# A decode block that reads 256 MB: a new load order, a re-fitted planner, and the q projection in row form

## The chip, the cores and the metric

One core of one Trainium2 chip. The metric is the device time of one execution in microseconds (us), the median of several; the profile is one execution with the hardware profiler. Several chips were used in turn, so every comparison is with the kernel before run in the same rounds on the same chip.

In the profile's lines PE is the tensor engine, PEld its weight loads, DVE VectorE, ACT ScalarE, and SPq the queue that issues the loads. `<-` names what ended a wait; "issue" is idle time for which the profile shows no such end. P.V is the product of the softmax's weights with V.

## The reference, cut to what matters

```python
def _A_ref(x, k_cache, v_cache, wq, wo):          # B=4, Sq=1, Hq=32, Hkv=8, Sk=8192, Dh=128
    q = (x @ wq).reshape(B, Sq, Hq, Dh).transpose(0, 2, 1, 3)
    scores = einsum("bhqd,bhkd->bhqk", q, repeat(k_cache, 4)) * Dh ** -0.5
    o = einsum("bhqk,bhkd->bhqd", softmax(scores), repeat(v_cache, 4))
    return o.transpose(0, 2, 1, 3).reshape(B, Sq, Hq * Dh) @ wo
def _B_ref(x, w_gate, w_up, w_down):
    return (silu(x @ w_gate) * (x @ w_up)) @ w_down

x = A_x
x = x + _A_ref(layernorm(x), K, V, wq, wo);  x = x + _B_ref(layernorm(x), ...)
x = x + _A_ref(layernorm(x), K, V, wq, wo);  x = x + _B_ref(layernorm(x), ...)   # the same K, V and weights
```

Both layers read the same caches. K and V are 134 MB in bf16, far more than the 15 slots of 1 MiB that the kernel has for them, so most of it is read twice.

## The kernel before

A cache unit is 1 MiB (half of one head's K or V). The pool has 11 slots of one unit; four more slots come from wq once the last q projection is done. The kernel lays itself out with a planner: steps (a matmul group, a transpose, an eviction) with estimated durations, dependencies, PSUM banks and slots; it simulates the engines and the load queue and emits the program in the order that comes out. The load order is a string. `K` and `P` are the next one or two K units, `a110` or `A11` a V unit or pair of layer 0, `b`/`B` of layer 1, and `c110` says that layer 1 uses the unit that layer 0 left in its slot (kept, not loaded again). `KM` K units of a batch are kept over to layer 1 as well.

```python
class Plan:
    HOP = 0.06
    PAGE = 5.0          # us from one block of 256 instructions to the next
    PAGE_N = 256
    LOAD_LEAD = 2.1
    LOAD_TAIL = 2.1
    ...
                s.start = t
                dma_at = max(dma_at, t + self.LOAD_LEAD) + s.us
                s.end = dma_at + self.LOAD_TAIL
ORDER = ("c100 c101 P c260 x P c300 c301 c261 wq P wg1 c120 P c340 P K K c341 P P wo1 A06 P wo0 P a010 K c240 "
         ... )
NSLOT = 11
KM = (4, 0, 0, 0)
```

The crossing of a batch (layer 0 to layer 1: output projection, layer norm, FFN, layer norm, q) has 128 matmuls for q in two halves of 16 heads. The weights are stationary (128x128), x moves with 4 columns:

```python
for h in heads:
    for kt in range(KT):
        matmul(ps[:, bk * BW + h * B:bk * BW + (h + 1) * B],
               lhsT=wq_sb[:, kt, h * Dh:(h + 1) * Dh], rhs=xnT[:, kt * B:(kt + 1) * B],
               start=(kt == 0), stop=(kt == KT - 1))
```

Scores are line 622 of the kernel before (648 after), the K transposes 606 (632), P.V in row form 763 (789) and by columns 748 (774), the FFN 809 and 873 (835 and 899), the q projection 472 (496).

Of the kernel before, what the change touches and what calls it, by code (L numbers as in the profile page):

```python
# [115 lines left out]
class Plan:  # L116

    HOP = 0.06
    PAGE = 5.0
    PAGE_N = 256  # L120
    LOAD_LEAD = 2.1
    LOAD_TAIL = 2.1

    def __init__(self, nslots, banks):
# [11 lines left out]
    def load(self, us, fn, slots, pair=None):  # L136
        s = Step("sp", us, fn, [], [0])
        s.slot_of, s.pair = slots, pair
        self.loads.append(s)
        return s  # L140

    def run(self):
        engines = ("pe", "dve", "act")
        free_at = {e: 0.0 for e in engines}
        todo = {e: [] for e in engines}
        waits = {}
        users = {}
        for s in self.steps:
            waits[s] = len(s.deps)
            for d in s.deps:  # L150
                users.setdefault(d, []).append(s)
            if not s.deps:
                todo[s.eng].append((0.0, s))
        bank_free = {b: 0.0 for b in self.banks}
        held = {}
        slots = [(0.0, i) for i in range(self.nslots)]
        li = 0
        sp_at = 1.0
        dma_at = 0.0
        done = []  # L160

        def finish(s):
            done.append(s)
            for u in users.get(s, ()):
                waits[u] -= 1
                if waits[u] == 0:
                    t = max(d.end + (self.HOP if d.eng != u.eng else 0.0) for d in u.deps)
                    todo[u.eng].append((t, u))

        def room(s):  # L170
            if s.slot_of is None:
                return 0.0, []
            if s.pair is None:
                return min(((f, [i]) for f, i in slots), default=None)
            at = {i: f for f, i in slots}
            return min(((max(f, at[i + 1]), [i, i + 1]) for i, f in at.items()
                        if i + 1 in at and i + 1 != self.nslots), default=None)

        def pump(now):
            nonlocal li, sp_at, dma_at, slots  # L180
            while li < len(self.loads):
                s = self.loads[li]
                t = sp_at
                got = room(s)
                if got is None:
                    return
                t = max(t, got[0])
                if s.slot_of is not None:
                    if t > now:
                        return  # L190
                    slots = [x for x in slots if x[1] not in got[1]]
                    for u, i in zip((s.slot_of, s.pair), got[1]):
                        self.slot[u] = i
                s.start = t
                sp_at = t + 0.35
                dma_at = max(dma_at, t + self.LOAD_LEAD) + s.us
                s.end = dma_at + self.LOAD_TAIL
                li += 1
                finish(s)

        pe_n = 0
        page_at = 0.0

        def fetched(at, s):
            nonlocal pe_n, page_at
            if s.eng != "pe" or s.n == 0:
                return at + s.us
            first, pe_n = pe_n, pe_n + s.n
            for k in range(first // self.PAGE_N + 1, pe_n // self.PAGE_N + 1):
                there = at + s.us * (k * self.PAGE_N - first) / s.n  # L210
                at += max(0.0, page_at + self.PAGE - there)
                page_at = max(there, page_at + self.PAGE)
            return at + s.us

        self.slot = {}
        left = len(self.steps)
        pump(0.0)
        while left:
            best = None
            for e in engines:  # L220
                cand = None
                for t, s in todo[e]:
                    if s.take is not None:
                        b = min(bank_free.values()) if bank_free else None
                        if b is None:
                            continue
                        t = max(t, b)
                    at = max(t, free_at[e])
                    k = (at > free_at[e] + 1e-9, at if at > free_at[e] + 1e-9 else 0.0, s.prio[0])
                    if cand is None or k < cand[0]:  # L230
                        cand = (k, at, s)
                if cand is not None and (best is None or cand[1] < best[0]):
                    best = (cand[1], cand[2])
            nxt = None
            got = room(self.loads[li]) if li < len(self.loads) else None
            if got is not None:
                nxt = max(sp_at, got[0])
            if best is None and nxt is None:
                raise RuntimeError("the plan is stuck")
            if best is None or (nxt is not None and nxt <= best[0]):  # L240
                pump(nxt)
                continue
            at, s = best
            s.start, s.end = at, fetched(at, s)
            free_at[s.eng] = s.end
            for i, (_, x) in enumerate(todo[s.eng]):
                if x is s:
                    todo[s.eng].pop(i)
                    break
            if s.take is not None:  # L250
                b = min(bank_free, key=lambda x: bank_free[x])
                del bank_free[b]
                held[s.take] = b
                self.bank[s.take] = b
            if s.free is not None:
                bank_free[held.pop(s.free)] = s.end + self.HOP
            if s.slot_of is not None:
                slots.append((s.end + self.HOP, self.slot[s.slot_of]))
            for i in range(s.gives):
                slots.append((s.end + self.HOP, self.nslots + i))  # L260
            left -= 1
            finish(s)
        while li < len(self.loads):
            raise RuntimeError("loads left")
        return max(s.end for s in self.steps)

    def emit(self):
        for s in sorted(self.steps + self.loads, key=lambda s: (s.start, s.prio[0])):
            s.fn()


ORDER = ("c100 c101 P c260 x P c300 c301 c261 wq P wg1 c120 P c340 P K K c341 P P wo1 A06 P wo0 P a010 K c240 "
         "K K a071 c121 a011 wg0 c031 K a070 a000 c370 P c371 a040 a001 a050 P wu0 a030 c030 a041 a051 P K K "
         "a020 K a031 a021 a150 wo2 a151 A17 wo3 wu1 wd0 wd1 a160 a161 a131 a130 K K K a121 K a110 a111 K K K "
         "K K K K K K K K b010 c241 a141 a120 b011 a140 a100 K K K K K b061 K K K K K K b060 a101 K b070 K K "
         "K b071 K c200 c201 b040 b041 b050 b051 b020 b001 b000 b021 K K K a250 c141 a251 K c140 K K K K K K "
         "K K K K K K a270 a271 a220 a221 a210 P K K P P A20 A26 A24 K A23 K K a211 K b151 b150 K K b160 K "
         "b170 K b171 c321 b161 b110 b130 b131 b111 K a330 a310 K K a360 K K K K K K a361 K K a331 K K K K K "
         "a320 a350 a351 a311 a300 a301 a341 a340 a321 A37 b230 b250 b231 b251 b220 b221 K K K K P K K K K K "
         "K K K K K b210 B27 b211 b360 b320 B35 B31 B33 b361 ")  # L280
NSLOT = 11
NP = 2
NQB = 1
LATE = (6, 3)
KM = (4, 0, 0, 0)
TAILSPLIT = True
MERGE = True

# [1 line left out]
def bass_interleave_layers__gqa_block_cached__swiglu_ffn__decode_kernel(  # L290
# [33 lines left out]
    with ExitStack() as es:  # L324
# [142 lines left out]
        def q_proj(heads, deps, tag):  # L467
# [8 lines left out]
                           reads=[f"wq{kt}", "xnT"], writes=[f"pb{bk}"], sig=(kt == KT - 1 and h == heads[-1]))  # L476
            return PL.add("pe", 0.029 * KT * len(heads), mm, deps, CHAIN, take=tag, n=2 * KT * len(heads))

        def q_spread(src, n, key, deps, tag):
            def mm():  # L480
                bk = pbk(tag)
# [46 lines left out]
        def q_half(b, hf, mm_tag, deps, prior):  # L528
# [2 lines left out]

            def scl():
                bk = pbk(mm_tag)
                src = ps[:, bass.ds(bk * BW + b + hf * nh * B, nh, step=B)]
                op("dve", lambda e: e.tensor_scalar(qT2[:, hf * nh:(hf + 1) * nh], src, qscale[:, b:b + 1], None,
                                                    op0=ALU.mult),
                   reads=[f"pb{bk}", "qscale"], writes=[f"qT2_{hf}"])
            s1 = PL.add("dve", 0.21, scl, deps, CHAIN, free=mm_tag)
            tag = f"qs{b}_{hf}"
            sp = q_spread(qT2[:, hf * nh:(hf + 1) * nh], nh, f"qT2_{hf}", [s1], tag)  # L540

# [20 lines left out]
        def load_two(u0, u1):  # L562
# [4 lines left out]
                      writes=[f"slot{k}_{h}" for k in (s, s + 1) for h in range(2)] +  # L567
                      ([f"wq{k - NSLOT}" for k in (s, s + 1)] if s >= NSLOT else []))
            home[u0], home[u1] = u0, u1
            return PL.load(4.914, fn, u0, u1)  # L570

        def load_pair(u):
            kind, l, b, g, cp = u
# [4 lines left out]
                      writes=[f"slot{s}_0", f"slot{s}_1"] + ([f"wq{s - NSLOT}"] if s >= NSLOT else []))  # L578
            home[u] = u
            if u != last_unit:  # L580
                return PL.load(2.505, fn, u)

            def half(h):
                s = PL.slot[home[u]]
# [309 lines left out]
        def chain(b, deps, prior):  # L894
# [6 lines left out]
            mm = None  # L901
            for hf in range(2):
                tag = f"q{b}_{hf}"
                mm = q_proj(range(hf * Hq // 2, (hf + 1) * Hq // 2), [cen, mm], tag)
                out_.append(q_half(b, hf, tag, [mm, qs], prior))
            if b == B - 1:
                mm.gives = KT
# [196 lines left out]
```

## Time and profile before

| | before |
|---|---|
| median | 638.8 us (638.27 to 640.04, 3 runs) |
| span of the profiled run | 636.9 us |
| read from HBM | 256.1 MB in 231 units and the weights |
| loads: first to last packet | 1.8 to 625.8 us |
| time of the data packets over 16 engines | 620.2 us |
| PE, DVE busy | 397 us, 403 us |

The row on data packets comes from the trace's records of single DMA packets. A window's loss, below, is always 8 us x (420 - its GB/s) / 420, with 420 as the rate of a full window of cache loads.

### The profile page before, as it was taken

How to read it: one execution, taken by the hardware profiler on the slowest of the kernel's cores; microseconds unless marked ns; L12 is line 12 of the kernel's file. 1: busy time of each engine (PE TensorE's matmuls, PEld its weight loads, DVE VectorE, ACT ScalarE, POOL GpSimd, SP SyncE). 2: the span in 40 equal slices, each digit the busy share in tenths (PEclk: the TensorE clock that was granted, in tenths of full speed). 3: DMA queues.
4: the chain of work that ended last, by engine and by line, in shares of the span. 5: the costliest groups of instructions: out<-in, count | busy, mean ns of one | idle time of the engine just before them, and what ended most of it. 6: DMA issues, size and time to landing. Idle time of an engine off the chain costs nothing.

```text
span 636.9 us, 18609 instructions
## 1 busy us (share of the span) xinstructions
PE 397.1 (62%) x8689; PEld 205.1 (32%) x8689; DVE 402.7 (63%) x615; ACT 40.4 (6%) x107; POOL 1.8 (0%) x8
## 2 busy tenths in 40 slices
PE   0375444454786675677576665578667676856686
PEld 0221211113542141135421241333431244721265
DVE  4477764365236958876579777366667863489832
ACT  1000200002000020000200100000100020000100
POOL 1000000000000000000000000000000000000000
PEclk9997686657557767667667778555575667568686
DMA  8999999999989999999999999999999999999991
GB/s 356 423 426 412 405 417 423 420 418 401 387 348 400 422 418 419 420 412 421 402 408 419 422 425 428 417 408 420 418 408 421 415 419 421 417 409 419 423 425 65
DMA packets 37237, 257.32 MB, mean 404 GB/s; under 512 B 3492, under 2 KB 9384, under 8 KB 10664
## 3 DMA queue, kind: packets, MB, share of 16 engines
q1 hardware_dynamic: 37160, 256.14, 97.7%
q8 instruction: 68, 1.11, 0.7%
q14 instruction: 9, 0.07, 0.0%
HBM read 256.12 MB, written 0.00 MB: 402 GB/s over the span
## 4 chain that ended last, share of the span: by engine, by line
DMA 63%; PE 18%; DVE 16%; issue 2%; SPq 0%; ACT 0%
DMA pool<-in_A_k_cache_dram 39%; DMA pool<-in_A_v_cache_dram 18%; DVE pool L606 12%; PE ps L622 7%; PE ps L763 5%; DMA wq_sb<-in_A_wq_dram 3%; PE ps L472 2%; DMA wo_sb<-in_A_wo_dram 2%; DMA wq_sb<-in_A_k_cache_dram 2%; DVE wq_sb L606 1%; PE ps L809 1%; PE ps L726 1%; DVE ps L790 1%; PE ps L681 1%; PE ps L873 1%
## 5 line engine op out<-in xcount | busy, mean ns | idle before, releaser
L606 DVE STREAM_TRANSPOSE pool<-pool 128x2048 uint32<-128x2048 uint32 x116 | 264.8, 2300 | 70.8 <-DMA pool<-in_A_k_cache_dram 70.6
L622 PE MATMUL ps<-pool,qpad 32*32 32x512 bf16 x3840 | 190.6, 543 | 127.2 <-DVE pool L606 120.7
L622 PEld LDWEIGHTS ps<-pool,qpad 32*32 32x32 bf16 x3840 | 54.6, 108 | 240.1 <-DVE pool L606 179.6
L763 PE MATMUL ps<-pool,pp 128*32 128x256 bf16 x1936 | 100.0, 366 | 43.1 <-DMA pool<-in_A_v_cache_dram 31.6
L763 PEld LDWEIGHTS ps<-pool,pp 128*32 128x32 bf16 x1936 | 57.5, 122 | 81.6 <-DMA pool<-in_A_v_cache_dram 42.8
L790 DVE STREAM_TRANSPOSE ps<-ps 128x256 f32<-128x256 f32 x62 | 28.4, 458 | 74.7 <-PE ps L763 74.4
L645 ACT ACTIVATE pp<-ps,negm 128x512 bf16<-128x512 f32 x32 | 21.6, 686 | 329.6 <-DVE negm L641 306.5
L726 PE MATMUL ps<-oT,wo_sb 128*128 128x4 bf16 x640 | 23.0, 167 | 12.6 <-DVE oT L794 9.2
L726 PEld LDWEIGHTS ps<-oT,wo_sb 128*128 128x128 bf16 x640 | 20.7, 103 | 24.7 <-DVE oT L794 16.7
L641 DVE TENSOR_REDUCE negm<-ps 128x1 f32<-128x512 f32 x32 | 19.9, 683 | 12.1 <-PE ps L622 12.1
L472 PE MATMUL ps<-xnT,wq_sb 128*128 128x4 bf16 x640 | 18.3, 166 | 12.1 <-DMA wq_sb<-in_A_wq_dram 11.4
L472 PEld LDWEIGHTS ps<-xnT,wq_sb 128*128 128x128 bf16 x640 | 17.7, 104 | 14.5 <-DMA wq_sb<-in_A_wq_dram 11.5
L606 DVE STREAM_TRANSPOSE wq_sb<-wq_sb 128x2048 uint32<-128x2048 uint32 x8 | 18.1, 2290 | 3.5 <-DMA wq_sb<-in_A_k_cache_dram 3.4
L681 PE MATMUL ps<-ident,pp 128*128 128x128 bf16 x128 | 16.0, 311 | 6.3 <-DVE pp L670 5.8
L622 PE MATMUL ps<-wq_sb,qpad 32*32 32x512 bf16 x256 | 13.2, 547 | 8.5 <-DVE wq_sb L606 8.5
L458 ACT ACTIVATE lnv<-var,eps_sb 128x4 f32<-128x4 f32 x10 | 3.0, 298 | 218.0 <-DVE var L453 218.0
L681 PEld LDWEIGHTS ps<-ident,pp 128*128 128x128 bf16 x128 | 12.7, 143 | 12.5 <-DVE pp L670 7.6
L792 DVE TENSOR_REDUCE osum<-ps 128x4 f32<-128x32 f32 x62 | 11.9, 191 | 2.1
L794 DVE TENSOR_TENSOR oT<-osum,invL 128x4 bf16<-128x4 f32 x62 | 10.5, 169 | 2.1
L670 DVE TENSOR_SCALAR pp<-pp,alpha 128x512 bf16<-128x512 bf16 x32 | 9.0, 346 | 1.8 <-ACT alpha L663 1.8
L690 ACT ACTIVATE pp<-ps 128x1024 bf16<-128x1024 bf16 x8 | 8.2, 1024 | 26.9 <-PE ps L681 26.9
L438 PE MATMUL ps<-xx,onesm 128*128 128x32 f32 x20 | 6.3, 410 | 5.3 <-DVE xx L433 4.3
(68 smaller groups left out, 149.4 us busy)
## 6 DMA issues: line engine op xcount, KB each, us to landing
pool<-in_A_k_cache_dram SPq DMA_DIRECT2D x86, 1024.0 KB, 9.7
pool<-in_A_v_cache_dram SPq DMA_DIRECT2D x82, 1024.0 KB, 10.0
pool<-in_A_k_cache_dram SPq DMA_DIRECT2D x15, 2048.0 KB, 15.8
pool<-in_A_v_cache_dram SPq DMA_DIRECT2D x10, 2048.0 KB, 16.6
wq_sb<-in_A_k_cache_dram SPq DMA_DIRECT2D x6, 1024.0 KB, 13.6
wq_sb<-in_A_wq_dram SPq DMA_DIRECT2D x1, 4096.0 KB, 22.0
wo_sb<-in_A_wo_dram SPq DMA_DIRECT2D x4, 1024.0 KB, 16.2
wq_sb<-in_A_k_cache_dram SPq DMA_DIRECT2D x1, 2048.0 KB, 10.3
```

Of the source, the lines that this page charges most:

```text
L472: op("pe", lambda e: e.matmul(ps[:, bk * BW + h * B:bk * BW + (h + 1) * B], lhsT=wq_sb[:, kt, h * Dh:(h + 1) * Dh], rhs=xnT[:, kt * B:(kt ...
L606: op("dve", lambda e: e.transpose(v, v), reads=keys, writes=keys)
L622: op("pe", lambda e: e.matmul(ps[32 * c:32 * (c + 1), a * BW:(a + 1) * BW], lhsT=qpad[rows, qbuf, es_, g, :], rhs=ap[h][rows, :, es_ // 2, ...
L641: op("dve", lambda e: e.tensor_reduce(negm[:, q, a:a + 1], bank(a), AX.X, ALU.max, negate=True), reads=[f"pb{a}"], writes=[f"negm{q}_{a}"])
L645: op("act", lambda e: e.activation(pblk(q)[:, :, a, :], bank(a).rearrange("p (t j) -> p t j", j=32), ACTF.Exp, bias=negm[:, q, a:a + 1], s ...
L670: op("dve", lambda e: e.tensor_scalar(seg, seg, alpha[:, q, a:a + 1], None, op0=ALU.mult), reads=[f"pp{q}_{a}", f"alpha{q}"], writes=[f"pp ...
L681: op("pe", lambda e: e.matmul(stg[:, t * P:(t + 1) * P], lhsT=pp[:, q, blk * P:(blk + 1) * P], rhs=ident[:], is_transpose=True, start=True ...
L726: op("pe", lambda e: e.matmul(ps[:, OPJ * BW + nq * B:OPJ * BW + (nq + 1) * B], lhsT=wo_sb[:, h, nq * P:(nq + 1) * P], rhs=oT[:, l, h, :], ...
L763: op("pe", lambda e: e.matmul(ps[32 * n:32 * (n + 1), bk * BW:bk * BW + 256], lhsT=pp[:, q, col:col + 32], rhs=v[:, 8 * f:8 * (f + 1), 32 ...
L790: op("dve", lambda e: e.transpose(blk, blk), reads=[f"pb{bk}"], writes=[f"pb{bk}"])
L792: op("dve", lambda e: e.tensor_reduce(osum[:], diag, AX.X, ALU.add), reads=[f"pb{bk}"], writes=["osum"])
L794: op("dve", lambda e: e.tensor_tensor(oT[:, l, g * REP:(g + 1) * REP, b], got, invL[:, q, g * REP:(g + 1) * REP], ALU.mult), reads=[f"pb{b ...
```

## The change

Three things at once. (1) The planner's load model is re-fitted: a load that is issued with little data ahead of it costs up to 1.05 us, and a block of instructions takes 5.8 us to come beside loads and 3.8 without. (2) A new order, found under that model: 34 paired loads instead of 27, 23 kept V units instead of 21, no kept K units. (3) The crossings' q projection in row form: x is stationary (4 columns), 512 columns of wq move; four column strips of the array write to four 32-row strips of one bank. A VectorE transpose in 32x32 blocks then puts q back into columns.

```diff
-    PAGE = 5.0
+    PAGE = 5.8
+    PAGE_IDLE = 3.8
-    LOAD_LEAD = 2.1
+    LOAD_LEAD = 2.0
+    LOAD_SOFT = 1.05
+    LOAD_EASE = 3.7
+    def late(self, ahead):
+        if ahead < self.LOAD_LEAD:
+            return max(self.LOAD_LEAD - ahead, self.LOAD_SOFT)
+        return max(0.0, self.LOAD_SOFT * (self.LOAD_EASE - ahead) / (self.LOAD_EASE - self.LOAD_LEAD))
-                dma_at = max(dma_at, t + self.LOAD_LEAD) + s.us
+                dma_at += self.late(dma_at - t) + s.us
...
-KM = (4, 0, 0, 0)
+KM = (0, 0, 0, 0)
+ORDER = ("c300 c120 c121 c030 c200 c031 c201 c301 wq x a051 P P a041 P c240 c321 wo1 c241 P P P c140 P a000 P " ...
+        def q_rows(hf, deps, tag):
+                ...                                         # cut
+                for kt in range(KT):
+                    w = wq_sb[:, kt, hf * nh * Dh:(hf + 1) * nh * Dh].rearrange("p (h d) -> p h d", d=Dh)
+                    for n in range(4):
+                        matmul(ps[32 * n:32 * n + B, bk * BW:(bk + 1) * BW], lhsT=xnT[:, kt * B:(kt + 1) * B],
+                               rhs=w[:, :, 32 * n:32 * (n + 1)], start=(kt == 0), stop=(kt == KT - 1),
+                               tile_position=(0, 32 * n))
+            return PL.add("pe", 1.88, mm, deps, CHAIN, take=tag, n=2 * 4 * KT)
...
-                src = ps[:, bass.ds(bk * BW + b + hf * nh * B, nh, step=B)]
+                blk = bank(bk).bitcast(mybir.dt.uint32)
+                op("dve", lambda e: e.transpose(blk, blk), reads=[f"pb{bk}"], writes=[f"pb{bk}"])
+                src = ps[:, bass.ds(bk * BW + b, nh, step=32)]
```

## The prediction

> **What bounds the kernel now.** I read the page's busy shares and 40 slices first, then its queue section and chain, then busy time by 8 us windows, then the waits of the queue that issues the loads, and last the end of the chain.
>
> The page, slices and queues:
>
> ```profile
> span 636.9 us, 18609 instructions
> PE 397.1 (62%) x8689; PEld 205.1 (32%) x8689; DVE 402.7 (63%) x615; ACT 40.4 (6%) x107; POOL 1.8 (0%) x8
> ...
> GB/s 356 423 426 412 405 417 423 420 418 401 387 348 400 422 418 419 420 412 421 402 408 419 422 425 428 417 408 420 418 408 421 415 419 421 417 409 419 423 425 65
> ...
> q1 hardware_dynamic: 37160, 256.14, 97.7%
> q8 instruction: 68, 1.11, 0.7%
> ```
>
> No compute engine is over 63%; the 16 DMA engines carry data 97.7% of the span. The bytes set the time. The chain says the same: 63% DMA, and its compute links are mostly short hops (transpose, scores) that let a buffer go so that the next load can start. So only four things can move the end: bytes, rate, stretches in which the load queue runs dry, and the tail after the last load.
>
> Busy time by windows (columns: PE, PEld, DVE, ACT, POOL busy us with counts, clock, DMA share, GB/s):
>
> ```profile
> 176.00:184.00 8.00, 5.90 (x196) 5.05 (x189) 2.29 (x11) 0.50 (x2) 0.00 (x0) 0.50 1.01 418
> 184.00:192.00 8.00, 7.02 (x168) 3.06 (x161) 3.36 (x5) 0.00 (x0) 0.00 (x0) 0.57 0.76 262
> 192.00:200.00 8.00, 3.81 (x136) 2.00 (x111) 3.52 (x2) 0.00 (x0) 0.00 (x0) 0.86 0.97 393
> ...
> 304.00:312.00 8.00, 4.57 (x120) 3.26 (x117) 2.23 (x9) 1.10 (x3) 0.00 (x0) 0.60 0.97 383
> ...
> 320.00:328.00 8.00, 4.71 (x88) 2.10 (x72) 4.08 (x4) 0.00 (x0) 0.00 (x0) 0.71 0.99 395
> ```
>
> A full window of cache loads moves about 420 GB/s. What a poor one lost is 8 us x (420 - rate)/420: 3.0 us at 184, 0.5 at 192, 0.7 at 304, 0.5 at 320. With 464 (397), 560 (403) and some smaller ones it comes to nearly 7 us. As a check: 256.1 MB at 420 GB/s is 609.8 us; the 5892 packets of 1 KB (the pieces of wo and w_down) take 50.2 ns each in the packet records where 1 KB at 420 GB/s over 16 engines would be 39.0, so 4.1 us more, and the 3.5 KB packets 0.5; sum 614.4. The data runs from about 2.5 us to 623: 620.5 us. The difference, 6.1 us, is the same loss found another way. The windows near 150 to 168 (370 to 398 GB/s) are those slow weight packets, not stalls.
>
> The waits of the issuing queue between 160 and 204 us say why it ran dry at 184:
>
> ```profile
> SPq L92 <- PE ps L622: 12.4, 3, 10.1
> SPq L62 <- PE ps L763: 10.2, 4, 8.8
> ```
>
> It waited for scores (L622) and for P.V (L763) to free slots. That is the first crossing: layer 0 of batch 0 ends, FFN, q projection, layer 1 begins. Six of the 11 pool slots were out of use then: four kept K units (KM = 4) and c030, c031.
>
> The chain at that crossing and at the end:
>
> ```profile
> 178.73 1.88 PE ps L472 x64
> 180.64 0.25 DVE qT L535
> 180.93 1.88 PE ps L472 x64
> 182.84 0.25 DVE qT L535
> ...
> 623.80 0.97 PE ps L748 x32
> ```
>
> The two halves of q go one after the other, PE then DVE. After the last pair lands at 623.75 the tail takes 13.1 us.
>
> **What the Trainium skill says.** (1) "DMA: Bandwidth & Descriptors", Specifications, gives 435 GB/s as the fabric ceiling, and its Rules for kernel authors want 128 partitions and at least 1 MiB per DMA. All cache loads here satisfy that, and the full slices show 417 to 428 GB/s, so no load shape has much left to win. (2) "Runtime: NRT & Kernel Launch", Instruction fetch mechanics: instructions come in 16 KiB blocks of 256 over the sequencer's own DMA queue. The trace agrees: 2 x 8689 PE instructions / 256 = 67.9, and queue 8 has 68 packets. The page calls crossing a block mostly hidden; the trace shows PE gaps of 2.2, 0.85 and 0.98 us with "issue" as their cause, so here it is not always hidden. (3) "Vector Engine (DVE) Microarchitecture Reference", 3.8: the 32x32 transpose sustains one element per cycle per lane. The trace has 458 ns for 128x256 and 2300 ns for 128x2048, a slope of 1.03 ns per column. (4) "TensorE: Matmul & The Clock Gate", Part 3: a narrow stationary operand may use a 32-column strip, and matmuls on several strips run together. The P.V rows at L763 do this already: 16 matmuls of 256 columns took 0.62 us in the densest stretches, 1.05 in slow ones.
>
> **The change, part by part.**
>
> Bytes. I counted the order strings. Before: 124 K units, 64 layer-0 V units, 43 layer-1 V units, 231 MiB in all (21 V units and 4 K units are reused). After: 128 + 64 + 41 = 233 (23 V units reused, KM all zero). Two more units: in the packet records a 1 MiB load is 128 packets x 316.2 ns / 16 engines = 2.53 us, so +5.06 us.
>
> Pairs. 27 before (16 P, 11 A and B), 34 after (19 + 15). A pair is 128 x 622.7 ns / 16 = 4.98 us against 2 x 2.53 = 5.06; 7 more save 0.55 us. Bytes and pairs together: +4.5 us. The planner's own load constants (4.924, 2.51) only change its bookkeeping.
>
> q projection. Of 512 matmuls and weight loads over four crossings 128 remain. PE loses 384 pairs = 768 instructions = 3 blocks; queue 8 should show 65. Its blocks took 1.07 us each on one engine: 3 x 1.07 / 16 = 0.2 us of DMA. PE time per half: 16 matmuls of 512 columns on four strips, twice L763's columns, so 1.24 to 2.1 us against 1.88 now. At the granted clock of 0.50 seen at the first crossing I take 2.0. No gain there. DVE gets eight transposes of 128x512: 458 + 256 x 1.03 = 0.72 us each, 5.8 us in all. DVE is 63% busy, but two per crossing lie in series: +1.4 us, and +0.2 from PE. Against that the 192 instructions fewer take off the fetch: 1003 instructions went through 160 to 184 us, 24 ns each, and two issue gaps of 0.85 and 0.98 lie in or just after this chain. I take 1.5 us back. The crossing itself is about even.
>
> Order and planner. The new model charges a load issued with under 3.7 us of data ahead and so prefers plans with a deeper queue. Where it shows: five V units retained for batch 0 and no K, so 6 free slots instead of 5 at the first crossing; 5 retained instead of 6 for batch 1. I take 3.0 of the 3.5 us at 184 to 200 as recovered and 1.7 of the other 3.3: -4.7 us. This is my least certain term. wq first lets q start near 18 us instead of 24, but no DMA time was lost there (423 to 431 GB/s from 8 to 32 us), so it buys only slots.
>
> Tail. The last pair is B35, by rows, instead of B33, by columns. Before, the PE worked 4.4 us from 623.80 to the residual add. After: two units of 0.62, the last unit's 1.0, two output projections of 0.57 and hand-overs, about 4.0. -0.4 us.
>
> Sum: 638.8 + 4.5 - 0.2 - 4.7 - 0.4 = 638.0 us.
>
> **Rivals.** (A) The stalls only move. Buffers are as many as before, crossings still hold 5 to 7 slots, batches 2 and 3 hold 6 and 7 as before, and a large pair must wait for two adjacent free slots, which the 7 extra pairs do more often. Then 6 to 7 us of stalls stay and the time is 642.5 to 643.5. For it: the queue waited for slots over 450 us in all, so small shifts matter. Against: the largest stall sits where the retained K units go away. (B) All stalls vanish: 638.8 + 4.3 - 6.8 - 0.4 = 636. The model was fitted for this, but the model before missed such stalls too. (C) DVE or PE becomes the bound: the K stretches run DVE 7.3 to 8.0 us of 8 and a transpose takes 2.3 us per unit against 2.5 us of load. 5.8 us of new DVE work and later K starts could push a stretch over. At worst some 3 us, 641.
>
> **Range and chances.** The two known terms (bytes and stalls) nearly cancel. The floor without any stall is near 636, a little less if loads run slightly faster: low 634.5. The high end is rival A with all stalls kept: 643. Two per cent is 12.8 us: a gain of it would need 626, about 10 us below the floor; a loss needs 8 us of new stalls on top of the old ones. Faster 0.01, within 2% 0.96, slower 0.03.
>
> **What would show it.** HBM read near 258.2 MB and 34 issues of 2 MiB; queue 8 at 65 packets; PE at 8305 matmuls; eight 128x512 transposes near 0.72 us; no 8 us window under 300 GB/s between 8 and 616 us; the span from last landing to the end near 12.7 us. I am wrong if the poor windows add up to over 7 us again, if the full windows leave 415 to 425 GB/s, or if the bytes don't grow.

## The result, and the profile after

The changed kernel takes 640.5 us (640.45 to 640.82, 4 runs), the kernel before 638.9 in the same rounds. The ratio is 1.0024, 95% interval 1.0007 to 1.0042. Ratios here are the mean time of one kernel's runs over that of the other's runs of the same rounds, so not quite the ratio of the medians. In later rounds the changed kernel gave 1.0025 (1.0011 to 1.0040). So it is slower by some 1.6 us: far within 2%, and clear of the noise.

The page of the changed kernel, slices and queues:

```profile
span 638.7 us, 17831 instructions
PE 403.8 (63%) x8305; PEld 192.7 (30%) x8305; DVE 417.6 (65%) x627; ACT 40.4 (6%) x107; POOL 1.8 (0%) x8
...
GB/s 361 424 410 422 424 420 428 409 413 378 361 419 419 422 418 421 419 420 417 422 419 419 420 429 421 423 424 411 397 395 423 418 415 420 417 422 419 430 420 74
...
q1 hardware_dynamic: 36440, 258.23, 97.9%
q8 instruction: 65, 1.06, 0.7%
```

8305 matmuls, 65 blocks and 258.2 MB are as foreseen. The dip in the slices before (348 at 175 to 191 us) is gone, but there is one of 361 at 160 to 175, and 397 and 395 at 447 to 479 where 418 and 408 stood.

Busy time by windows of the changed kernel (columns as in the prediction):

```profile
168.00:176.00 8.00, 5.12 (x104) 2.57 (x108) 2.24 (x8) 0.00 (x0) 0.00 (x0) 0.50 0.78 286
440.00:448.00 8.00, 7.51 (x207) 5.97 (x200) 3.71 (x17) 0.75 (x3) 0.00 (x0) 0.50 1.00 402
448.00:456.00 8.00, 6.19 (x108) 3.00 (x104) 3.21 (x13) 0.50 (x2) 0.00 (x0) 0.71 0.99 382
456.00:464.00 8.00, 2.00 (x77) 1.29 (x80) 4.86 (x11) 2.97 (x9) 0.00 (x0) 0.72 1.00 411
464.00:472.00 8.00, 7.18 (x130) 3.31 (x130) 7.28 (x12) 1.02 (x1) 0.00 (x0) 0.64 0.98 385
472.00:480.00 8.00, 3.76 (x82) 1.22 (x90) 6.47 (x3) 0.00 (x0) 0.00 (x0) 0.78 1.00 407
```

The first line is the stall of the first crossing, 2.6 us lost where the kernel before lost 3.5 in two windows. The other five lost 2.2 us together (2.3 in the repeat after_again); the same windows of the kernel before lost 0.5 or so. The losses before near 304 and 320 us (1.2) are gone.

The balance, from packet records:

| us | before | after | difference |
|---|---|---|---|
| time of the data packets over 16 engines | 620.2 | 623.5 | +3.3 |
| first to last packet of the loads | 624.0 | 625.9 | +1.9 |
| so: stalls and overlaps | | | -1.4 |
| last packet to the end of the span | 11.1 | 10.9 | -0.2 |
| span | 636.9 | 638.7 | +1.8 |

Two more units, less what the pairs save, cost 3.3 us, and the stalls gave back only 1.4.

Why the load queue still ran dry is in its own waits between 140 and 180 us, and in the chain of the changed kernel there (start, duration, what):

```profile
SPq L62 <- PE ps L789: 19.6, 2, 17.4
```

```profile
158.13 0.85 PE ps L835 x26
158.98 2.35 issue
161.32 0.23 PE ps L835 x2
...
165.07 1.91 PE ps L496 x16
167.00 0.74 DVE ps L559
167.77 0.25 DVE qT L561
168.06 1.91 PE ps L496 x16
169.99 0.74 DVE ps L559
...
172.31 1.93 PE ps L789 x32
```

The last loads before the gap were issued by 156 us: four loads, two of them pairs, so six units or about 15 us of data. The next slot could come only from P.V (L789), and P.V stood behind the whole crossing, which went from 153.5 to 172.3 us. So the queue waited 17.4 us in one piece, of which what had been issued before covered all but the 2.6 us lost. The second half of q starts only when the first has been transposed and scaled (0.74 and 0.25 us).

The new transpose itself is as estimated (a group's count, busy us, mean ns, then idle before):

```profile
L559 DVE STREAM_TRANSPOSE ps<-ps 128x512 uint32<-128x512 uint32 x8 | 5.8, 720 | 4.2 <-PE ps L496 4.2
```

### The profile page after: what moved, and what is told of

Same layout as the page of the kernel before. It is cut to its first block, busy times and chain, and to the rows that moved or that the text cites. A ratio compares the mean times of both kernels' runs of the same rounds, so it can differ in the third digit from the quotient of the medians.

```text
span 638.7 us, 17831 instructions
## 1 busy us (share of the span) xinstructions
PE 403.8 (63%) x8305; PEld 192.7 (30%) x8305; DVE 417.6 (65%) x627; ACT 40.4 (6%) x107; POOL 1.8 (0%) x8
## 4 chain that ended last, share of the span: by engine, by line
DMA 60%; PE 16%; DVE 16%; SPq 5%; issue 2%; ACT 0%
DMA pool<-in_A_v_cache_dram 31%; DMA pool<-in_A_k_cache_dram 24%; DVE pool L632 11%; PE ps L789 6%; PE ps L648 5%; SPq L92 5%; DMA wo_sb<-in_A_wo_dram 3%; DMA wq_sb<-in_A_k_cache_dram 2%; DVE wq_sb L632 2%; PE ps L835 1%; PE ps L707 1%; PE ps L496 1%; PE ps L752 1%; DVE ps L816 1%; PE ps L899 0%
## 5 line engine op out<-in xcount | busy, mean ns | idle before, releaser
L632 DVE STREAM_TRANSPOSE pool<-pool 128x2048 uint32<-128x2048 uint32 x120 | 273.5, 2299 | 61.2 <-DMA pool<-in_A_k_cache_dram 61.0
L648 PE MATMUL ps<-pool,qpad 32*32 32x512 bf16 x3840 | 201.9, 554 | 133.1 <-DVE pool L632 128.1
L648 PEld LDWEIGHTS ps<-pool,qpad 32*32 32x32 bf16 x3840 | 54.8, 110 | 258.4 <-DVE pool L632 193.9
L789 PE MATMUL ps<-pool,pp 128*32 128x256 bf16 x1952 | 100.9, 365 | 43.6 <-DMA pool<-in_A_v_cache_dram 39.1
L789 PEld LDWEIGHTS ps<-pool,pp 128*32 128x32 bf16 x1952 | 57.2, 121 | 81.1 <-DMA pool<-in_A_v_cache_dram 48.6
L632 DVE STREAM_TRANSPOSE wq_sb<-wq_sb 128x2048 uint32<-128x2048 uint32 x8 | 18.1, 2291 | 3.0 <-DMA wq_sb<-in_A_k_cache_dram 3.0
L648 PE MATMUL ps<-wq_sb,qpad 32*32 32x512 bf16 x256 | 12.7, 527 | 7.3 <-DVE wq_sb L632 7.3
L496 PE MATMUL ps<-wq_sb,xnT 128*4 128x512 bf16 x128 | 12.8, 547 | 1.6 <-DVE qT L561 1.1
L835 PE MATMUL ps<-xnT,wu_sb 128*128 128x4 bf16 x280 | 9.1, 166 | 4.3 <-issue 3.4
L835 PEld LDWEIGHTS ps<-xnT,wu_sb 128*128 128x128 bf16 x280 | 8.3, 104 | 7.1 <-issue 5.2
L835 PE MATMUL ps<-xnT,wg_sb 128*128 128x4 bf16 x280 | 8.2, 166 | 2.3 <-DVE xnT L456 1.7
```

What stands on the lines that cost most here:

```text
L496: op("pe", lambda e: e.matmul(ps[32 * n:32 * n + B, bk * BW:(bk + 1) * BW], lhsT=xnT[:, kt * B:(kt + 1) * B], rhs=w[:, :, 32 * n:32 * (n + ...
L632: op("dve", lambda e: e.transpose(v, v), reads=keys, writes=keys)
L648: op("pe", lambda e: e.matmul(ps[32 * c:32 * (c + 1), a * BW:(a + 1) * BW], lhsT=qpad[rows, qbuf, es_, g, :], rhs=ap[h][rows, :, es_ // 2, ...
L789: op("pe", lambda e: e.matmul(ps[32 * n:32 * (n + 1), bk * BW:bk * BW + 256], lhsT=pp[:, q, col:col + 32], rhs=v[:, 8 * f:8 * (f + 1), 32 ...
L835: op("pe", lambda e: e.matmul(ps[:, bk * BW + (fo - f0) * B:bk * BW + (fo - f0 + 1) * B], lhsT=w_sb[:, kt, fo * P:(fo + 1) * P], rhs=xnT[: ...
```

## The experiments

Theory S: the load stream sets the time, as bytes plus stalls; a longer crossing means a longer stall. Rivals: the gain or loss is in instruction fetch (F), in the planner's constants (M), or in the pairs. All twelve runs gave correct results. "Packets" is the time of the data packets over 16 engines, "loads end" the last packet of a load, both of the profiled run.

| run | ratio to before | 95% | MB | packets | loads end |
|---|---|---|---|---|---|
| before | 1 | | 256.1 | 620.2 | 625.8 |
| changed kernel | 1.0024 | 1.0007 to 1.0042 | 258.2 | 623.5 | 627.8 |
| after_again | 1.0025 | 1.0011 to 1.0040 | 258.2 | 624.1 | 628.0 |
| after_old_q | 1.0046 | 1.0034 to 1.0059 | 258.2 | 624.5 | 628.4 |
| order_only | 1.0049 | 1.0037 to 1.0062 | 258.2 | 623.9 | 628.4 |
| model_only | 1.0016 | 1.0003 to 1.0029 | 256.1 | 620.4 | 625.8 |
| q_only | 1.0093 | 1.0080 to 1.0107 | 256.1 | 620.3 | 631.7 |
| before_no_kept_k | 1.0125 | 1.0111 to 1.0139 | 260.3 | 630.5 | 634.1 |
| after_no_pairs | 1.0052 | 1.0039 to 1.0066 | 258.2 | 626.9 | 629.3 |
| after_fetch_shift | 1.0014 | 1.0001 to 1.0028 | 258.2 | 623.9 | 627.7 |
| q_same_plan | 0.9990 | 0.9978 to 1.0003 | 256.1 | 620.4 | 625.5 |
| q_same_plan_shift | 0.9990 | 0.9976 to 1.0003 | 256.1 | 620.6 | 626.1 |
| after_interleaved | 1.0022 | 1.0009 to 1.0034 | 258.2 | 623.2 | 627.2 |
| searched_order | 0.9970 | 0.9957 to 0.9984 | 257.2 | 620.0 | 623.8 |

One thousandth is 0.64 us.

### The parts alone

**The old q projection under the new order and planner.**

```diff
-                mm = q_rows(hf, [cen, mm], tag)
+                mm = q_proj(range(hf * Hq // 2, (hf + 1) * Hq // 2), [cen, mm], tag)
# and the column source without the transpose, 0.21 us instead of 0.98
```

> The changed kernel with the old q projection of the crossings (x moving, 128 matmuls a crossing, no transposes); order and planner new. Theory S (the load stream sets the time; the row form of q puts 1.6 us more in series into each crossing, and the loads that wait for it stall longer): the crossing's q part shrinks from 7.2 to about 5.6 us, the poor window near 168 to 176 us loses 1 to 1.6 us less, the time falls to about 639.3 (638.5 to 639.8). Rival F (instruction fetch: the 192 instructions a crossing saved are worth more than the transposes): the time rises by about 1.3 us, to 641.8, which is also what the new planner's own arithmetic says (638.0 against 636.7).

641.2 us against 638.05: 1.0046. Theory S missed here. The first crossing did get shorter, by 2.5 us to the spread of q, and its window lost 0.9 us instead of 2.6 (first line below). Only 1.1 of the 2.5 us lie in the q part itself (5.5 us instead of 6.6); the rest is a gap in the FFN that this run does not have, of which more under "Block boundaries moved". A new loss came at 296 us (0.7), and 440 to 480 lost 2.9 instead of 2.2:

```profile
168.00:176.00 8.00, 5.31 (x122) 3.35 (x119) 2.03 (x8) 0.00 (x0) 0.00 (x0) 0.50 0.94 375
296.00:304.00 8.00, 3.66 (x90) 2.40 (x78) 4.65 (x17) 0.00 (x0) 0.00 (x0) 0.71 1.00 381
...
456.00:464.00 8.00, 4.33 (x106) 2.56 (x103) 4.46 (x11) 2.24 (x7) 0.00 (x0) 0.50 1.01 379
```

So under this order the row form seems worth about 1.3 us (1.0046 against 1.0024 and 1.0025, but the intervals overlap), in the direction of rival F. The gain doesn't come at the first crossing, where the row form is a loss. Where it comes is not shown: the windows from 168 to 616 us lost 3.8 us net here, 3.9 in the changed kernel and 4.1 in its repeat. That it is instruction fetch at the later crossings is not shown either: the planner also laid those stretches out differently.

**The new order alone.**

```diff
-ORDER, KM of before
+ORDER, KM of after        # planner constants and q projection as before
```

> The kernel before with the new load order and without kept K units; its planner and its q projection unchanged. Theory S: bytes cost +4.0 (two units more, seven pairs more), the stall at the first crossing shrinks from 3.6 to 1 to 2 us, so about 639.5 to 640.5, and HBM read is 258.2 MB. Rival M (the planner constants, not the order, carry the loss): at or under 638.9. If the order is the whole change, 640.5.

641.35 us, 1.0049, a little over what was expected. The order with its two units carries the whole loss and more. Its windows lost 1.2 us at 168 and 3.0 from 440 to 480.

**The new planner constants alone.**

```diff
-    PAGE = 5.0, LOAD_LEAD = 2.1, loads 2.505 and 4.914
+    PAGE = 5.8 / 3.8, LOAD_LEAD = 2.0, LOAD_SOFT, LOAD_EASE, late(), loads 2.51 and 4.924
```

> The kernel before with the new planner constants alone; order, kept K units and q projection unchanged, so the same 256.1 MB. Theory S: same bytes, only the interleaving on the engines differs, 638 to 640.5. Rival M (the new planner judges rightly): it puts this plan 3.8 us behind the changed kernel (640.5 against 636.7 in its own arithmetic), so it should measure about 644.

639.0 us, 1.0016: rival M falls. The new constants alone, with the same bytes, make the kernel some 1.0 us slower, clear of the noise. By its own arithmetic the new planner put this layout 3.8 us behind the changed kernel; measured, it is half a microsecond ahead of it (1.0016 against 1.0024, intervals that overlap). Whatever the new constants fit better, they don't rank these two layouts.

**The row form alone, with the planner told of it.**

> The kernel before with the row form of q alone; order, kept K units and planner unchanged, 256.1 MB. Theory S: +1.6 us in series at each crossing, so the stall at 184 grows by 1 to 1.6 us: 640 to 640.8 if nothing else moves. But the old planner, which sees the 0.77 us of each transpose, lays the program out anew and its own arithmetic has a hole of 7.3 us in the loads near 365 us: if that hole is real, about 647 to 648. Rival F (fetch relief outweighs): under 638.5.

644.4 us, 1.0093, below the 647 to 648 that was forecast with the hole and above what was forecast without it. The hole that the old planner's arithmetic had near 365 us is real; the windows of this run:

```profile
360.00:368.00 8.00, 3.79 (x72) 2.49 (x73) 5.73 (x22) 3.08 (x9) 0.00 (x0) 0.75 0.77 317
368.00:376.00 8.00, 7.16 (x141) 6.14 (x138) 4.08 (x16) 1.02 (x1) 0.00 (x0) 0.61 0.51 172
```

6.7 us lost in two windows that were full before. 0.77 us more in eight steps made the planner choose another layout, in which the queue waited for P.V for 11.2 us. The planner foresaw this hole (7.3 us); it did not get differences of one to three us right.

**The row form with the layout held.** The planner keeps the old durations and counts, so each engine has the old order. The diff is against the run above:

```diff
-            return PL.add("pe", 1.88, mm, deps, CHAIN, take=tag, n=2 * 4 * KT)
+            return PL.add("pe", 0.029 * KT * nh, mm, deps, CHAIN, take=tag, n=2 * KT * nh)
-            s1 = PL.add("dve", 0.98, scl, deps, CHAIN, free=mm_tag)
+            s1 = PL.add("dve", 0.21, scl, deps, CHAIN, free=mm_tag)
```

> The kernel before with the row form of q, but the planner is told the old durations and instruction counts, so every engine has the order of the kernel before and only the q instructions differ. It tells the row form apart from the new layout that the planner made of it when q alone was changed (644.4). If the loss there was the layout (the hole near 365 us): the hole is gone. If the row form is a gain as it was under the new order (1.4 us): 637 to 638. If the 1.6 us in series at the first crossing outweigh it: 639 to 640.5, with the stall at 184 to 200 us up from 3.6 to about 5.

638.07 us against 638.54: 0.9990, not clear of equal. The hole is gone, so it was the layout. At the first crossing the second spread of q comes 2 us later than before (185.81 against 183.76) and the stall grew in its window (below: 3.6 us lost, 3.0 before), but the next window is full again (416, where 393 stood), so the two together lost 3.6 us, not the 5 that one forecast had. About 1.2 of the 2 us came back right after: the first scores ran in one piece (186.03 to 187.94), where the kernel before had 0.98 us of "issue" in the middle of them (183.98 to 187.06; last two lines below, before and here). The prediction had counted on such a relief from fewer instructions. The losses at 304 and 320 us moved to 288 and 296 (0.9 us together). By itself the row form is worth somewhere between -0.2 and +1.4 us here.

```profile
184.00:192.00 8.00, 6.54 (x204) 3.44 (x201) 4.46 (x8) 0.00 (x0) 0.00 (x0) 0.69 0.65 233
192.00:200.00 8.00, 3.24 (x107) 1.83 (x103) 3.19 (x2) 0.00 (x0) 0.00 (x0) 0.95 1.01 416
...
186.01 1.05 PE L622 MATMUL ps<-pool,qpad 32*32 32x512 bf16 x16 [0.98 <-issue]
186.03 1.91 PE L639 MATMUL ps<-pool,qpad 32*32 32x512 bf16 x32
```

### Bytes against slots, and pairs

**No kept K units in the kernel before.**

```diff
-KM = (4, 0, 0, 0)
+KM = (0, 0, 0, 0)
```

> The kernel before with no K unit kept over the first crossing (four units loaded again, order, planner and q projection unchanged). It prices bytes against slots. If bytes set the time at 2.5 us a unit: +10.1 us of loads, less the stall at 184 to 200 us (3.6 us lost before, which should vanish as 9 instead of 5 slots are free there): 638.0 + 6.5 = 644.5, range 643.5 to 646.5, HBM read 260.3 MB. Rival (slots, not bytes, are what is short, so freeing four of them pays for the loads): 641 or less.

646.7 us against 638.6: 1.0125, 8.0 us, just over the range. The packets rose by 10.3 us for four units, 2.6 each. The stall at the crossing did go:

```profile
184.00:192.00 8.00, 5.62 (x176) 3.79 (x177) 6.36 (x6) 0.00 (x0) 0.00 (x0) 0.50 1.02 420
```

This is the trade of the change in its plainest form. Four free slots at the first crossing give back 3.4 us there, some of which is lost again at 256 to 288 us, and cost 10. A kept unit saves 2.6 us of packets; a stall that it causes has to be larger than that.

**No pairs in the changed kernel.** All `P`, `A`, `B` tokens split in two.

> The changed kernel with all 34 pairs issued as two loads of 1 MiB each in the same place. If a pair is worth what its packets say (4.94 us against 5.06, 0.12 each): +4 us, so 644.5. If the pairs make the new poor windows at 440 to 480 us (two adjacent slots have to be free at once), those windows recover 1 to 2 us and the time is 642 to 643, or below.

642.1 us, 1.0052, 1.8 us slower than the changed kernel by the ratios. The packets took 3.4 us more (16 KB packets take 617 ns in the changed kernel, two of 8 KB 632), so 34 pairs are worth 0.1 us each in the stream and half of it in the end; the first crossing's stall was smaller (359 GB/s instead of 286). The poor windows from 440 on stayed at 2.0 us. Pairs do not make them.

### Where the stalls of the changed kernel come from

**Block boundaries moved.** 64 idle transposes before x arrives:

```diff
+            for i in range(64):
+                matmul(xb[:, 64:192], lhsT=ident, rhs=ident, is_transpose=True)
```

> The changed kernel with 64 idle transposes of the identity put on the tensor engine before x arrives (it has nothing else to do then), so that every later block of 256 instructions begins 128 instructions earlier in the program; the plan, the loads and the waits are unchanged. If the 2.35 us gap in the FFN of the first crossing comes from a block boundary at that place and the crossing's length sets the stall at 168 to 176 us: the gap leaves that place, the window loses 0.5 to 1.5 us instead of 2.6, and the time falls by 0.5 to 2 us unless boundaries at later crossings now fall badly. If the gap has another cause, it stays where it is, and the time stays within 0.5 us of the changed kernel's.

639.8 us, 1.0014. The 2.35 us gap in the FFN's up projection is gone, the P.V after q began at 171.0 instead of 172.3, and the window at 168 lost 1.3 us instead of 2.6. So at this place a crossing shorter by 1.3 us made the stall shorter by as much. What is left is 1.38 us ahead of the down projection. The profile calls it "issue" too, but it is the wait for w_down: its last packet ended at 159.93 us, 0.6 us before the first of those matmuls. In the changed kernel that packet ended at 159.89, so there the gap cost 1.3 us and not 2.35.

That moving the boundaries did it is not shown. after_old_q has the same matmuls as the changed kernel up to this gap, with no boundary moved, and the gap is gone there too (second line; the first is this run):

```profile
160.53 1.63 PE L899 MATMUL ps<-hT,wd_sb 128*128 128x4 bf16 x56 [1.38 <-issue]
160.49 1.64 PE L897 MATMUL ps<-hT,wd_sb 128*128 128x4 bf16 x56 [1.32 <-issue]
```

after_interleaved, below, has the same (1.31 us; P.V at 170.95). What goes with the gap is the time of one block on queue 8: its packet began at 158.9 us in the changed kernel and at 158.8 and 158.6 in after_again and order_only, which have the gap, and at 155.2 in the two runs without it. So the gap is very likely a wait for that block; why it comes 3.7 us later in some programs than in others stays open.

In the time only some 0.6 us arrived, within the two intervals: from 440 to 480 this run lost 2.9 us instead of 2.2. The same shift under the old order, in the row form with its layout held, changed nothing:

> The same with the 64 idle transposes ahead of x, so all block boundaries lie 128 instructions earlier in the program. If where the boundaries fall is worth what it was under the new order, the time differs from the run without them by 0.3 to 1 us, in either direction; the gaps put down to issue move. If boundaries don't matter, it is the same within 0.3 us.

638.15 us against 638.07 without, both 0.9990, though the gaps put down to issue moved (one of 1.8 us now stands before a spread of q). So in that layout where the boundaries fall is worth little in the sum.

**K and V in turn beside the third crossing.** The order before mixed K units among the V units there; the new one has four K units before a row of 12 V loads. The queue's waits from 430 to 490 us say what that changes (the changed kernel, then the kernel before):

```profile
SPq L62 <- PE ps L789: 30.2, 11, 8.8
SPq L62 <- PE ps L648: 22.0, 8, 5.6
...
SPq L62 <- PE ps L622: 32.3, 12, 5.5
SPq L62 <- PE ps L763: 19.9, 12, 3.7
```

It waits for P.V (L789, L763) where it waited for scores (L648, L622), and up to 8.8 us at a time.

```diff
-... A22 A25 K K K K a260 A20 a261 b160 b161 b111 b170 b100 b150 b171 b101 b151 K K K
+... A22 A25 a260 A20 a261 b160 K K b161 K b111 K b170 b100 b150 b171 b101 b151 K K K
```

> The changed kernel with the last four K units of layer 0, batch 3, issued between the V units that follow (the row of 12 V units beside the third crossing becomes 4, then K and V in turn), as the order before had it. If that row, whose slots only the tensor engine frees while it also carries the crossing, makes the poor windows at 440 to 480 us: they lose under 1.2 us instead of 2.4, and the time falls by about 1 us to 639.5. The planner's own arithmetic says +0.5 us (641.0); if the poor windows come from something else, it is that or more.

639.75 us, 1.0022 against 1.0024: no gain. The windows from 440 to 480 did recover, to 0.3 us, and the waits for P.V there fell to 18.1 us in all and 4.3 at most, so the row of V loads was their cause: slots that only P.V frees, on a tensor engine that was busy up to 7.5 of 8 us at half clock with the crossing. But a new stall came ahead of them:

```profile
432.00:440.00 8.00, 6.06 (x136) 3.05 (x136) 6.58 (x9) 0.25 (x1) 0.00 (x0) 0.50 0.89 349
```

1.4 us lost there, 0.4 at 408 and 0.5 at 512. The stall moved, as rival A of the prediction had it. The first crossing, which the edit does not touch, lost 1.5 us here instead of 2.6, along with the block of the section above, which came early. From 312 to 616 us, where the edit acts, the windows lost 2.0 us net and 1.4 in the changed kernel: by itself the edit is a small loss, as the planner's arithmetic had it.

### A version that beats both

The runs point to: the row form with the layout held from it, the old planner, kept K units. From there I searched the order with the old planner, some 21,000 steps, scored at two load lags at once (2.1 and 2.9 us). It keeps four K and 20 V units (232 units, one more than before) and has 41 pairs. The three shared PSUM banks are zeroed at the start, because the transpose reads rows that no matmul wrote.

```diff
+        op("dve", lambda e: e.memset(ps[:, 4 * BW:7 * BW], 0.0), writes=["pb4", "pb5", "pb6"])
+ORDER = ("c261 wu0 x wq K c260 P K K wo2 K P P P wg0 P K P P c340 wo1 P K c101 c341 wg1 K wo0 P c240 c120 A00 K "
+         "c121 A06 A07 c370 P K A01 P K A05 c371 a031 wo3 A04 a151 A02 a030 a150 a160 c301 A17 K a161 wu1 K K K "
+         "wd1 wd0 c100 A13 a110 a111 K K b031 K c201 K K K K P P c030 c241 c300 P b061 P P b060 K A12 B01 P A14 K "
+         "K K A10 K b070 K K K b071 K b040 b041 b020 b021 b050 b000 b001 b051 K K K K a230 a231 K K K K K K c321 "
+         "K K K K K K a270 c140 a220 a221 K c200 a271 K K K a210 K P K K A24 A20 a260 A25 K P a261 K b110 a211 "
+         "b150 b151 K K c141 b170 K b111 b171 b161 b160 b130 b131 K K a330 a331 K K K K K K K K K K K K K K a351 "
+         "a350 a310 a360 a311 A30 a371 a370 a361 A32 A34 b230 b250 b251 b231 b220 b221 K K K K P K K K K K K K K "
+         "K K b210 B27 b211 b330 b320 b360 b361 B31 b350 b351 b331 ")
```

> The changed kernel once more, unaltered, in the same rounds as the next run, because it was measured against the kernel before on another chip than the experiments. If its place was not a matter of the chip: ratio 1.002 to 1.003 of the kernel before.

640.7 us, 1.0025, as in the first comparison.

> A try at a version that beats both: the row form of q, kept from the planner as in the run with the same plan; a load order found by some 21000 steps of search with the old planner, scored by the mean of its own time at two load lags (2.1 and 2.9 us) so as not to lean on one constant; four kept K units; three 16 KB-row pairs in four more places, 41 pairs and one unit more than the kernel before (20 V units kept, not 21); the three shared PSUM banks are zeroed first, as the transpose reads rows that no matmul wrote. The planner gives it 630.9 against 632.2 for the kernel before. If its arithmetic holds for an order it was searched on: 1.3 us under q_same_plan, 636.5 to 637. If a searched order loses what it was credited with, as the changed kernel did (credited with 3.8 us over the old order by its own planner, measured 1.6 us behind): 638 to 641.

(Its list of differences names the pairs clumsily: it means 41 pairs, 14 more than before.) 636.8 us against 639.1: 0.9970, ahead of the kernel before by 1.9 us and of the changed kernel by 3.5, by the ratios and clear of both; it is the first of the two forecasts (636.5 to 637). One unit more, yet its packets took as long as before: it has 14 more pairs, and the 16 KB packets took 618 ns instead of 623. The stall at the first crossing lost 1.4 us instead of 3.5 (window below); the loads end at 623.8.

```profile
184.00:192.00 8.00, 6.22 (x208) 3.59 (x216) 5.25 (x6) 0.00 (x0) 0.00 (x0) 0.71 0.89 346
```

It is one candidate, tried once. Which of its many differences matters was not taken apart.

## Why the prediction was right or wrong

The time, 640.5, lies in the range (634.5 to 643) and within 2%, as given at 0.96. The middle, 638.0, was 2.5 us low, and the sign against 638.8 was wrong: predicted -0.8, measured +1.6. That the error is no larger is in part luck: bytes and pairs were put 1.2 us too high, which hides part of the 3.3 us by which the recovered stalls were put too high.

- **What bounds it: right.** Bytes plus stalls explain the runs: each of the two numbers was moved and the time followed (four units no longer kept: packets +10.3 us, stall at the crossing -3.4, time +8.0; the hole of q_only: 6.7 us of stall, time +5.9). The 1.3 us of after_old_q are not explained by it. The prediction's check of its stalls does not hold: it let the data run from 2.5 to 623 us, but the packets run from 1.8 to 625.8, so that difference is 9.6 us and not 6.1. The larger figure also holds what is lost at the start, at the end and in the slow weight packets, so the two counts are not the same loss.
- **Bytes and pairs: +4.5, measured +3.3** in packets. Counts and MB were exact; the 16 KB packets took 617 ns in this run and not 623.
- **Blocks, instructions, transposes: right.** 65 blocks, 8305 matmuls, 720 ns, a half of q 1.9 us.
- **The crossing: half right.** +1.6 us in series came in full: q to the second spread took 5.0 us before (178.73 to 183.76) and 6.6 after (165.07 to 171.68). The 1.5 us that fewer instructions should give back did not come there: the largest gap, 2.35 us, fell in the FFN, ahead of the instructions that had been removed. With the old layout held, 1.2 of them did come (q_same_plan). Over the whole kernel the row form is worth about 1.3 us under the new order and 0.6 under the old one, and neither is clear of the noise.
- **Recovered stalls, -4.7: this is the step that failed**, the one called least certain. In its place the runs show -1.4. At the first crossing 1.0 of 3.5 us came back, not 3.0: one free slot more does not cover a stretch of 18.8 us in which nothing frees a slot (153.5 to 172.3). Some 1.1 us of the 2.6 lost there go with the late block: after_interleaved, which has the same crossing without it, lost 1.5. It was also treated as if it could only get better elsewhere, "1.7 of the other 3.3"; the losses at 304 and 320 went, but 2.2 us stood at the third crossing (0.5 before), from the row of V loads. The order string, read for its neighbours and not only counted, would have shown that row.
- **Tail: -0.4, measured -0.2** from the last packet.
- **Rival A (stalls only move)** was nearer than the main line in the stalls (none gained, against 1.4 measured and 4.7 predicted), if not in the time: part moved, as the third crossing and the interleaved run show. **B** is refuted. **C** is not seen for VectorE but for one window, 464 to 472 us, where its time went from 5.67 to 7.28 us and the loss from 0.4 to 0.7; how much of the third crossing's loss is the tensor engine's load rather than the order of the loads, no run separates.
- The signs named beforehand worked: one window under 300 GB/s (286) stands where none should.

What stays open: whether the row form gains at the later crossings and how, and why one block of instructions comes 3.7 us later in some programs than in others that are the same up to there.

## What to carry to other kernels

Where loads fill the span, price a byte first (here 2.6 us of packets a unit) and a stall second; a change that buys slots with bytes must remove more stall than it loads. A stall of a load queue is the longest stretch in which nothing frees a buffer, less the loads that were issued ahead of it. Buffers do cover it when there are enough (four more slots took the first crossing's stall away, one did not), but here they were paid for in bytes; a shorter stretch is not. A planner that searches on its own arithmetic can find the layouts that it is wrong about: hold the layout when you test an instruction change, and score a search at more than one value of its constants.

## What the Trainium skill lacked or had wrong

- "Runtime: NRT & Kernel Launch", Instruction fetch mechanics, calls crossing a 16 KiB block mostly hidden. Here the tensor engine sat idle for 2.35 us in a crossing while a block came late (packet at 158.9 us); where that block came at 155.2 it did not. The closest that blocks came was mostly 6.0 to 6.4 us apart beside loads (29.3, 35.7, 41.7, 47.9 us before) and 3.6 to 3.8 when the DMA engines were half idle or less (183.4, 187.2 before; 622.5, 626.1 after). The page has no such rate.
- "DMA: Bandwidth & Descriptors", Rules for kernel authors, asks for at least 1 MiB per DMA. Rates of larger single transfers stand on the skill's pages; what a larger load gains in a stream with others queued behind it does not. Here 2 MiB loads (16 KB per partition) took 617 to 623 ns per packet and 1 MiB loads 316 ns per half of it, so 1.5 to 2.5% more rate; 34 pairs were worth 1.8 us in the end.
- The same page has nothing on the rate of a load queue that keeps waiting for slots. Two such windows of the kernel before (304 and 320 us), whose DMA share was still 0.97 and 0.99, moved 383 and 395 GB/s instead of 420: part of a stall doesn't show as idle engines.
